# Two pairs of high and low tiles for queries and keys, and three more weight slots

## The chip, the core and the metric

The kernel runs on one core of one Trainium2 chip. The metric is the device time of one execution in microseconds (us). The engines are TensorE (PE: matmuls and transposes; PEld is its loading of weights), VectorE (DVE), ScalarE (ACT), GpSimd (POOL) and SyncE (SP), which here only issues DMAs. Each engine executes its own instructions strictly in the order in which the program lists them, so an instruction that waits holds up all that stand behind it on its engine.

## What is computed

An attention layer is followed by two feed-forward layers, all in float32. Queries, keys and values are 4 batches of 8 heads of 576 positions of 64 numbers; the attention's output is seen as 2304 tokens of 512 numbers.

```python
q_rot, k_rot = (rotate(q), rotate(k))            # cos and sin of the position
scores = scale * np.matmul(q_rot, k_rot.transpose(0, 1, 3, 2))
scores = scores - np.max(scores, axis=-1, keepdims=True)
attn = np.exp(scores)
attn = attn / (np.sum(attn, axis=-1, keepdims=True) + 1e-09)
x = np.matmul(attn, v)                           # then 2304 x 512
h = x @ w_in;  r = np.maximum(h, 0.0)            # w_in 512 x 2048
x = (s * (r * r) + b) @ w_out
g = x @ w_gate                                   # 512 x 1536
out = (g * (1.0 / (1.0 + np.exp(-g))) * (x @ w_val)) @ w_out2
```

## The kernel before

Every float32 factor is split into a high part (rounded to the format `F32R` that TensorE multiplies fast) and a low part (the rest), and a product is made of three matmuls: high by high, high by low, low by high. The high part is always made by ACT, a copy, and the low part by DVE or POOL, a subtraction.

**Attention** goes over 16 pairs of heads (`p` = 0 to 15). `prep(p)` prepares a pair: SP loads queries and keys into a tile `x` (two buffers); POOL rotates them in place (L486, L488, L491, L494); PE transposes them in three groups of three (L514) into PSUM tiles `pst`, which come from the same three PSUM buffers (`t`) as the transposes of the exponentials (L680, L683, `ps_t`); ACT writes the high parts of each group to `qkhi` (L523), and DVE the low parts to `qklo` (L525). When all three groups are done, ten DMAs on SP (L547, "the spread" below) lay `qkhi` and `qklo` out as the operands `a`, `t` and `kz` of the score matmuls. There are two sets of these operands, for even and odd pairs, so the spread of pair p can only start when the scores of pair p - 2 are done. Pairs 0 and 1 go without `qkhi` and a spread.

`pair(p)` has nine score tiles: PE multiplies (L619, `ps_s`, two PSUM buffers), DVE takes the maximum (L622, `nm`), and ACT the exponential (L626, `e`). In three thirds, the exponentials are transposed by PE, split by ACT (`ph`, L688) and DVE (`pl`, L695), and multiplied by the values (L710, L712); ACT copies the result out (L723, `xr`), and SP stores it (L731). So each pair has nine maxima on DVE and nine exponentials on ACT, by which the places in their programs are counted below.

The feed-forward weights come as 8-byte numbers. A conversion takes one ACT instruction (L304), three on DVE (L307, L310, L315), one on ACT for the high part (L342) and one for the low part (L349), on POOL for the first `WA` weights and on DVE for the others. The first `WA` weights go to slots of the pool `wa`, and they may be converted while attention still runs. When attention is done, its pools are given up, and the pool `wb` with `WB` slots takes their memory.

**The order** of the instructions comes from a planner, the class `Schedule`. Every operation has an engine, an assumed duration, a priority (a smaller number goes first) and tokens for the buffers that it takes and gives back; `sch.free` says how many buffers of each kind there are. The planner plays the program through with the assumed durations; on each engine it takes the ready operation with the best priority whose buffers are free. The chip then executes that order, with semaphores for the true dependences. The preparation of pair p has priority 100 p - 240, and unit u of pair p 100 p + 10 u. The token of `qkhi` and `qklo` is taken by the first transpose of a pair and given back when its ten spread DMAs have landed:

```python
acq = (ps_tok, hi_tok if p > 1 else tok) if g == 0 else (ps_tok,)
...
return sch.dma(
    256 * o.shape[1], lambda: nc.sync.dma_start(out=o.bitcast(F32), in_=i().bitcast(F32)), pr + 6, (*trs, *zeros[z]),
    (tok,) if first else (), (hi_tok,), pace=1.3
)
```

All DMAs of the kernel are issued on SP (`nc.sync`) and a few on ACT (`nc.scalar`), none on POOL.

Of the kernel before, what the change touches and what calls it, by code (L numbers as in the profile page):

```python
# [9 lines left out]
F32R = mybir.dt.float32r  # L10
# [154 lines left out]
def t_pool(n):  # L165
    return 2.35e-3 * n + 0.08
# [11 lines left out]
def tile_attention_moe_moe(  # L178
# [16 lines left out]
    nc = tc.nc  # L195
    B, H, S, D = q.shape
# [8 lines left out]
    NU = PC  # L205
    QA = PC // 2
    UBS = (512, 512, 512, 384, 384)
    WA = 10
    WB = 22
    NE = 7  # L210
    LATE, LAST = 1 << 20, 1 << 21
    WARM = 75
# [9 lines left out]
    sch = Schedule()  # L222
    op = sch.op
    sch.free.update({
        "raw": 3, "dec": 2, "wa": WA, "x": 2, "vr": 2, "ry": 1, "hi": 1, "vh": 3, "opb0": 1, "opb1": 1, "l": 2, "lb": 2, "cr": 1, "e": NE, "ph": 2, "pl": 2,
        "xr": 2, "rbx": 1, "s": 2, "t": 3, "v": 1, "xhb": 1, "gb": 2, "rb2": 3,
    })

# [1 line left out]
    dram = ctx.enter_context(tc.tile_pool(name="dram", bufs=1, space=DRAM))  # L230
    wa_p = ctx.enter_context(tc.tile_pool(name="wa", bufs=WA))
    raw_p = ctx.enter_context(tc.tile_pool(name="raw", bufs=3))
# [13 lines left out]
    att = ExitStack()  # L246
    at_c = att.enter_context(tc.tile_pool(name="at_c", bufs=1))
    ld_p = att.enter_context(tc.tile_pool(name="ld", bufs=2))
    vr_p = att.enter_context(tc.tile_pool(name="vr", bufs=2))
    rp_p = att.enter_context(tc.tile_pool(name="rp", bufs=1))  # L250
    v_p = att.enter_context(tc.tile_pool(name="v", bufs=3))
    ph_p = att.enter_context(tc.tile_pool(name="ph", bufs=2))
    pl_p = att.enter_context(tc.tile_pool(name="pl", bufs=2))
# [170 lines left out]
    def prep(p):  # L424
# [6 lines left out]
        st = {} if p else first_st  # L431
# [24 lines left out]
        def views2(a):  # L456
            return st["x"].rearrange("p c j (a d) -> p c j a d", a=2)[:, :, :, a], st["ry"][:, :, :, a]
# [4 lines left out]
        for g in range(G):  # L462
            cs = slice(g * PC // G, (g + 1) * PC // G)
            eng = "dve" if p == 0 else "pool"
            e = nc.vector if eng == "dve" else nc.gpsimd
            tt = t_dve if eng == "dve" else t_pool
            wide = [128, PC // G, 2, D // 2]
            def views(a, cs=cs):
                return st["x"].rearrange("p c j (a d) -> p c j a d", a=2)[:, cs, :, a], st["ry"][:, cs, :, a]
            def r0(g=g, e=e, views=views, cs=cs, wide=wide):  # L470
                if g == 0:
                    st["ry"] = rp_p.tile([128, PC, 2, 2, D // 2], F32, tag="ry", name="ry")
                e.tensor_tensor(out=views(0)[1], in0=views(1)[0], in1=rt[:, cs, 2:3].to_broadcast(wide), op=ALU.mult)
            def r1(e=e, views=views, cs=cs, wide=wide):
                e.tensor_tensor(out=views(1)[1], in0=views(0)[0], in1=rt[:, cs, 1:2].to_broadcast(wide), op=ALU.mult)
            def r2(e=e, cs=cs):
                xv = st["x"].rearrange("p c j (a d) -> p c (j a) d", a=2)[:, cs]
                e.tensor_tensor(out=xv, in0=xv, in1=rt[:, cs, 0:1].to_broadcast([128, PC // G, 4, D // 2]), op=ALU.mult)
            def r3(e=e, cs=cs):
                xv = st["x"].rearrange("p c j d -> p c (j d)")[:, cs]  # L480
                e.tensor_tensor(out=xv, in0=xv, in1=st["ry"].rearrange("p c j a d -> p c (j a d)")[:, cs], op=ALU.add)
            o = st.get("rope")
            if o is None and p:
                def y0():
                    st["ry"] = rp_p.tile([128, PC, 2, 2, D // 2], F32, tag="ry", name="ry")
                    nc.gpsimd.tensor_tensor(out=views2(0)[1], in0=views2(1)[0], in1=rt[:, :, 2:3].to_broadcast(whole), op=ALU.mult)  # L486
                def y1():
                    nc.gpsimd.tensor_tensor(out=views2(1)[1], in0=views2(0)[0], in1=rt[:, :, 1:2].to_broadcast(whole), op=ALU.mult)  # L488
                def y2():
                    xv = st["x"].rearrange("p c j (a d) -> p c (j a) d", a=2)  # L490
                    nc.gpsimd.tensor_tensor(out=xv, in0=xv, in1=rt[:, :, 0:1].to_broadcast([128, PC, 4, D // 2]), op=ALU.mult)  # L491
                def y3():
                    xv = st["x"].rearrange("p c j d -> p (c j d)")
                    nc.gpsimd.tensor_tensor(out=xv, in0=xv, in1=st["ry"].rearrange("p c j a d -> p (c j a d)"), op=ALU.add)  # L494
                n2 = PC * D
                for y, fn in enumerate((y0, y1, y2, y3)):
                    o = op("pool", t_pool(n2 if y < 2 else 2 * n2), fn, pr, (o, *lds[0], *rt_op), (ry_tok,) if y == 0 else (), (ry_tok,) if y == 3 else ())
                st["rope"] = o
            elif not p:
              o = None  # L500
              for y, fn in enumerate((r0, r1, r2, r3)):
                deps = [o, *lds[g], rt_op[g]]
                if y == 0 and g > 0:
                    deps.append(st["first"])
                o = op(eng, tt(fd if y > 1 else fd // 2), fn, pr + g, deps, (ry_tok,) if y == 0 and g == 0 else (),
                       (ry_tok,) if y == 3 else (), port=eng == "dve")
                if y == 0 and g == 0:
                    st["first"] = o
            ps_tok = Token("t")
            def tr(g=g):  # L510
                st["ps", g] = ps = ps_t.tile([128, 512], F32, tag="t", name="pst")
                rv = st["x"].rearrange("p c j d -> p c (j d)")
                for c in range(PC // G):
                    nc.tensor.transpose(taken(ps)[:, :, c * 64:(c + 1) * 64], rv[:, g * (PC // G) + c], ident.rearrange("p (h r) -> p h r", h=2))  # L514
            acq = (ps_tok, hi_tok if p > 1 else tok) if g == 0 else (ps_tok,)
            prt = pr + 3 + g
            o = st["tr"] = op("pe", 0.33, tr, prt, (o, eye_op, st.get("tr"), *(zeros[z] if p < 2 else ())), acq, (x_tok,))
            if p > 1:
                def hi(g=g):
                    if g == 0:  # L520
                        st["hi"] = rp_p.tile([128, 2 * S], F32R, tag="hi", name="qkhi")
                        st["lo"] = rp_p.tile([128, 2 * S], F32R, tag="lo", name="qklo")
                    nc.scalar.activation(out=place(st["hi"], g), in_=taken(st["ps", g]), func=AF.Copy, scale=qs_t)  # L523
                def lo(g=g):
                    nc.vector.scalar_tensor_tensor(  # L525
                        out=place(st["lo"], g), in0=taken(st["ps", g]), scalar=qs_t, in1=place(st["hi"], g).bitcast(F32), op0=ALU.mult, op1=ALU.subtract
                    )
                o = st["hi0"] = op("act", t_act(CG, True, 1), hi, prt, (o, qs_op, st.get("hi0")))
                trs.append(op("dve", t_dve(CG, 2), lo, prt, (o,), (), (ps_tok,)))
            else:  # L530
                def act(dst, rows, g=g):
                    scale = D ** -0.5 if rows is up else 1.0
                    return lambda: nc.scalar.activation(out=place(dst, g), in_=taken(st["ps", g])[rows], func=AF.Copy, scale=scale)
                def sub(dst, src, rows, g=g):
                    scale = D ** -0.5 if rows is up else 1.0
                    return lambda: nc.vector.scalar_tensor_tensor(
                        out=place(dst, g), in0=taken(st["ps", g])[rows], scalar=scale, in1=place(src, g).bitcast(F32), op0=ALU.mult, op1=ALU.subtract
                    )
                o1 = op("act", t_act(CG), act(t[dn], dn), prt, (o,))
                o2 = op("act", t_act(CG), act(a[up], up), prt, (o,))  # L540
                ops += [o1, o2, op("dve", t_dve(CG), sub(a[dn], a[up], up), prt, (o2,), (), (ps_tok,))]
                ops.append(op("act", t_act(CG), act(kz[up], dn), prt, (o,), (), (ps_tok,)))
                ops.append(op("dve", t_dve(CG), sub(t[up], t[dn], dn), prt, (o1,), (), (ps_tok,)))
# [355 lines left out]
    def switch():  # L899
        att.close()  # L900
        pool("wb", WB)

# [14 lines left out]
    n_att = len(sch.ops)  # L917
    for z in range(WA):
        weight(("out" if z % 2 else "in", z // 2), ("wa",), TP * NP, after=s_turns[WU0 + WUS * z:][:1])
    sw = op("sp", 0.0, switch, LATE - 1, [o for o in sch.ops[:n_att] if o not in ends])  # L920
    sw2 = op("sp", 0.0, switch_2, LATE - 1, [sw, *ends])
    for z in range(WA, 2 * F1):
        weight(("out" if z % 2 else "in", z // 2), ("wb", "wc"), LATE + 12 * (z - WA), sw, lo_eng="dve")

# [446 lines left out]
```

## Time and profile before

| | us |
|---|---|
| median of 3 runs | 1133.07 |
| lowest, highest | 1133.0, 1134.01 |
| span of the profiled execution | 1130.5 |
| median less that span | 2.6 |
| PE busy in the span | 1103.6 |
| DVE busy | 801.2 |
| ACT busy | 591.0 |
| POOL busy | 193.0 |

The page has no time of its own for the profiled execution but its span, from the first to the last instruction; the 2.6 us are what the median has beyond it. The scores of attention run until about 303 us of the span, and its last products with the values start at 314 us; after that only feed-forward work is left. A matmul's end is modelled in the profile, so a busy PE need not be at its peak.

### The profile page before, as it was taken

Reading aid. Unit: us, or ns where it says so; the run is one execution under the profiler, and the core shown is the slowest. Engines: PE = TensorE matmul, PEld = TensorE weight load, DVE = VectorE, ACT = ScalarE, POOL = GpSimd, SP = SyncE. Lnnn points to the kernel's source line nnn. Section 1 sums busy time; section 2 is a strip of 40 time slices with the busy share of each in tenths; the row PEclk is TensorE's granted clock in tenths of the full one; section 3 lists DMA queues with packets and bytes.
Section 4 is the critical chain, followed back from the end, with each engine's and each line's share of the span. In section 5 each row is a group of like instructions: output and inputs, shape, how many; then the busy total and the mean of one; then the engine's idle time right before and its main releaser. Section 6 shows DMA issues by size and latency. Waiting matters only on the chain. (4 is left out here: it accounts for less than half of the span.)

```text
span 1130.5 us, 17993 instructions
## 1 busy us (share of the span) xinstructions
PE 1103.6 (98%) x6314; PEld 1006.8 (89%) x6314; DVE 801.2 (71%) x1391; ACT 591.0 (52%) x1199; POOL 193.0 (17%) x156
## 2 busy tenths in 40 slices
PE   8989989999999999999999999999999999999998
PEld 7889888989988788888899999999979999899986
DVE  5879788999979867868768764555565555655560
ACT  5979888889978845544554543322242222422230
POOL 6876775752210000000000000000000000000000
PEclk9899999999999999999999999999999999999999
DMA  5587978777375477576576766766646652666501
GB/s 117 128 208 175 240 184 213 175 184 185 89 235 185 128 227 235 177 238 225 198 241 212 254 224 207 245 204 204 210 160 220 196 195 97 196 229 197 181 10 46
DMA packets 185721, 211.16 MB, mean 187 GB/s; under 512 B 71824, under 2 KB 121120, under 8 KB 185632
## 3 DMA queue, kind: packets, MB, share of 16 engines
q1 hardware_dynamic: 183792, 209.23, 61.8%
q8 instruction: 50, 0.82, 0.3%
q10 hardware_dynamic: 1840, 0.79, 0.2%
q14 instruction: 39, 0.32, 0.1%
HBM read 142.07 MB, written 47.26 MB: 167 GB/s over the span
## 5 line engine op out<-in xcount | busy, mean ns | idle before, releaser
L1241 DVE TENSOR_TENSOR tmp<-hb,tmp 128x384 f32<-128x384 f32 x252 | 140.0, 557 | 113.3 <-PE hb L811 112.4
L811 PE MATMUL hb<-xh,w 128*128 128x384 f32 (+1 forms) x560 | 199.2, 356 | 1.0 <-DVE w L349 1.0
L809 PE MATMUL hb<-xh,w 128*128 128x384 f32 (+1 forms) x560 | 199.0, 355 | 0.3 <-DVE pl L695 0.3
L810 PE MATMUL hb<-xl,w 128*128 128x384 f32 (+1 forms) x560 | 198.8, 355 | 0.0
L809 PE MATMUL acc<-gh,w 128*128 128x512 f32 (+1 forms) x320 | 117.8, 368 | 0.0
L810 PE MATMUL acc<-gl,w 128*128 128x512 f32 (+1 forms) x320 | 117.6, 368 | 0.0
L811 PE MATMUL acc<-gh,w 128*128 128x512 f32 (+1 forms) x320 | 117.6, 367 | 0.0
L622 DVE TENSOR_REDUCE nm<-ps_s 128x1 f32<-128x576 f32 x144 | 108.0, 751 | 9.8 <-PE ps_s L619 8.6
L809 PEld LDWEIGHTS hb<-xh,w 128*128 128x128 f32 x560 | 105.1, 188 | 10.9 <-PE ps_t L683 0.5
L810 PEld LDWEIGHTS hb<-xl,w 128*128 128x128 f32 x560 | 105.1, 188 | 10.3
L811 PEld LDWEIGHTS hb<-xh,w 128*128 128x128 f32 x560 | 105.1, 188 | 9.8 <-DVE w L349 1.8
L626 ACT ACTIVATE e<-ps_s,nm 128x576 f32<-128x576 f32 x144 | 107.3, 746 | 8.4 <-DVE nm L622 7.8
L688 ACT ACTIVATE ph<-ps_t 128x512 fp32r<-128x512 f32 x192 | 106.2, 574 | 10.1 <-PE ps_t L680 7.8
L619 PE MATMUL ps_s<-t,a 128*128 128x288 f32 x320 | 101.2, 332 | 7.2 <-ACT e L626 7.0
L710 PE MATMUL ps_av<-ph,vh 128*128 128x384 f32 (+1 forms) x320 | 97.9, 327 | 0.7 <-ACT xr L723 0.6
L695 DVE TENSOR_TENSOR pl<-ps_t,ph 128x512 fp32r<-128x512 f32 x144 | 95.9, 683 | 2.5 <-ACT ph L688 1.4
L1256 ACT ACTIVATE tmp<-tmp 128x384 f32<-128x384 f32 x72 | 37.8, 525 | 111.1 <-DVE tmp L1241 108.9
L680 PE MATMUL ps_t<-ident,e 128*128 128x128 f32 x576 | 87.7, 279 | 5.6 <-DVE qklo L525 4.0
L619 PE MATMUL ps_s<-kz,a 128*128 128x288 f32 x320 | 90.8, 299 | 0.0
L810 PE MATMUL hb<-w 128*128 128x384 f32 x264 | 88.9, 337 | 0.0
L811 PE MATMUL hb<-w 128*128 128x384 f32 x264 | 88.8, 337 | 0.0
L809 PE MATMUL hb<-w 128*128 128x384 f32 x264 | 88.5, 335 | 0.0
(117 smaller groups left out, 2304.2 us busy)
## 6 DMA issues: line engine op xcount, KB each, us to landing
w<-wd SPq DMA_DIRECT2D x120, 512.0 KB, 4.3
wd<-w SPq DMA_DIRECT2D x48, 512.0 KB, 3.6
raw<-in_moe_w_out_dram SPq DMA_DIRECT2D x28, 512.0 KB, 4.1
x_d<-xr SPq DMA_DIRECT2D x64, 144.0 KB, 2.7
w<-wd SPq DMA_DIRECT2D x36, 256.0 KB, 3.6
raw<-in_moe_w_in_dram SPq DMA_DIRECT2D x16, 512.0 KB, 4.4
raw<-in_moe_w_gate_dram SPq DMA_DIRECT2D x12, 512.0 KB, 5.5
raw<-in_moe_w_val_dram SPq DMA_DIRECT2D x12, 512.0 KB, 6.6
```

Of the source, the lines that this page charges most:

```text
L619: nc.tensor.matmul(ps[:, hf * 512:hf * 512 + HS], a[:, q0:q0 + 128], m[:, k0:k0 + HS], start=y == 0, stop=y == len(todo) - 1)
L622: nc.vector.tensor_reduce(out=st["nm"][:, u:u + 1], in_=st["s", u], axis=AX.XY, op=ALU.max, negate=True)
L626: nc.scalar.activation(out=st["e", u].rearrange("p (f n) -> p f n", f=2), in_=st["s", u], func=AF.Exp, bias=st["nm"][:, u:u + 1], accum_ou ...
L680: nc.tensor.transpose(ps[:, z * 128:z * 128 + 128], st["e", u][:, kc * 128:kc * 128 + 128], ident)
L688: nc.scalar.activation(out=st["ph", y][0:rows, 512 * i:512 * i + n], in_=st["pt", y, i][0:rows, 0:n], func=AF.Copy)
L695: nc.vector.tensor_tensor(out=dst, in0=st["pt", y, i][0:rows, 0:n], in1=st["ph", y][0:rows, c].bitcast(F32), op=ALU.subtract)
L710: nc.tensor.matmul(ps, vv, st["ph", y][:, c], start=kc == 0, stop=kc == 4)
L809: nc.tensor.matmul(o, lh, rh, start=first, stop=False)
L810: nc.tensor.matmul(o, lh, rl, start=False, stop=False)
L811: nc.tensor.matmul(o, ll, rh, start=False, stop=last)
L1241: nc.vector.tensor_tensor(out=st[dst, f], in0=ps[z], in1=st[a, f], op=ALU.add)
L1256: nc.scalar.activation(out=st[key, f], in_=st[key, f], func=AF.Silu)
```

## The change

The tiles `qkhi` and `qklo` move from the pool `rp` (one buffer) to a pool `hi` of their own with two buffers each, and the planner's count of them goes from 1 to 2. The pool `wa` gets 11 slots in place of 10, and `wb` 24 in place of 22. The memory comes from `dynamic_dma_scratch_size`, by which the program keeps 1 KB of each partition for DMA descriptors in place of 16. A pair of `qkhi` and `qklo` has 9 KB of a partition, a weight slot 4 KB. From line 251 on, lines of the changed kernel have a number that is higher by one.

```diff
-    WA = 10
-    WB = 22
+    WA = 11
+    WB = 24
...
-        "raw": 3, "dec": 2, "wa": WA, "x": 2, "vr": 2, "ry": 1, "hi": 1, "vh": 3, "opb0": 1, "opb1": 1, "l": 2, "lb": 2, "cr": 1, "e": NE, "ph": 2, "pl": 2,
+        "raw": 3, "dec": 2, "wa": WA, "x": 2, "vr": 2, "ry": 1, "hi": 2, "vh": 3, "opb0": 1, "opb1": 1, "l": 2, "lb": 2, "cr": 1, "e": NE, "ph": 2, "pl": 2,
...
     rp_p = att.enter_context(tc.tile_pool(name="rp", bufs=1))
+    hi_p = att.enter_context(tc.tile_pool(name="hi", bufs=2))
...
-                        st["hi"] = rp_p.tile([128, 2 * S], F32R, tag="hi", name="qkhi")
-                        st["lo"] = rp_p.tile([128, 2 * S], F32R, tag="lo", name="qklo")
+                        st["hi"] = hi_p.tile([128, 2 * S], F32R, tag="hi", name="qkhi")
+                        st["lo"] = hi_p.tile([128, 2 * S], F32R, tag="lo", name="qklo")
...
-    nc = _bacc.Bacc("TRN2", target_bir_lowering=False, num_devices=1)
+    nc = _bacc.Bacc("TRN2", target_bir_lowering=False, num_devices=1, dynamic_dma_scratch_size=1024)
```

Since the planner has other counts, it gives out another order in all of attention. On ACT, before, the three parts of `qkhi` of pair 8 (`qkhi_2047`) stand around the fifth exponential of pair 6 (the exponentials with `nm_1908`):

```order
L626 ACTIVATE e_1966,l_1371<-ps_s_1930,nm_1908 128x576
L688 ACTIVATE ph_1960<-ps_t_1968 128x512
L688 ACTIVATE ph_1960<-ps_t_1978 128x512
L626 ACTIVATE e_1998,l_1371<-ps_s_1955,nm_1908 128x576
L626 ACTIVATE e_2015,l_1371<-ps_s_1989,nm_1908 128x576
L723 ACTIVATE xr_1928<-ps_av_1941 128x384
L688 ACTIVATE ph_1960<-ps_t_2017 64x384
L523 ACTIVATE qkhi_2047<-pst_2037,qs_203 128x2x192
L523 ACTIVATE qkhi_2047<-pst_2043,qs_203 128x2x192
L626 ACTIVATE e_2066,l_1371<-ps_s_2021,nm_1908 128x576
L523 ACTIVATE qkhi_2047<-pst_2050,qs_203 128x2x192
L688 ACTIVATE ph_2088<-ps_t_2073 128x512
```

On ACT of the changed kernel, `qkhi` of pair 8 (`qkhi_1845`) stands around the seventh exponential of pair 5 (`nm_1642`):

```order
L627 ACTIVATE e_1764,l_1393<-ps_s_1736,nm_1642 128x576
L724 ACTIVATE xr_1697<-ps_av_1709 128x384
L689 ACTIVATE ph_1707<-ps_t_1767 64x384
L689 ACTIVATE ph_1803<-ps_t_1791 128x512
L627 ACTIVATE e_1811,l_1393<-ps_s_1775,nm_1642 128x576
L689 ACTIVATE ph_1803<-ps_t_1815 128x512
L627 ACTIVATE e_1832,l_1393<-ps_s_1798,nm_1642 128x576
L524 ACTIVATE qkhi_1845<-pst_1835,qs_206 128x2x192
L524 ACTIVATE qkhi_1845<-pst_1841,qs_206 128x2x192
L627 ACTIVATE e_1866,l_1393<-ps_s_1826,nm_1642 128x576
L524 ACTIVATE qkhi_1845<-pst_1854,qs_206 128x2x192
L724 ACTIVATE xr_1697<-ps_av_1787 128x384
```

So it moved ahead by seven of the nine exponentials of a pair. From pair 7 to 15 it is seven for every pair, within one, and the nine transposes on PE and the three `qklo` on DVE move with it.

On DVE, before, the end of the last pair's maxima (`nm_4327`) has two instructions of weight conversions among twelve:

```order
L622 TENSOR_REDUCE nm_4327<-ps_s_4456 128x1
L695 TENSOR_TENSOR pl_4476<-ps_t_4450,ph_4461 128x512
L310 SCALAR_TENSOR_TENSOR dec_4316<-raw_4046,dec_4316 128x512
L695 TENSOR_TENSOR pl_4476<-ps_t_4468,ph_4461 128x512
L622 TENSOR_REDUCE nm_4327<-ps_s_4479 128x1
L695 TENSOR_TENSOR pl_4476<-ps_t_4487,ph_4461 128x512
L622 TENSOR_REDUCE nm_4327<-ps_s_4496 128x1
L307 TENSOR_SCALAR dec_4448<-dec_4448 128x512
L695 TENSOR_TENSOR ph_4461<-ps_t_4503,ph_4461 64x384
L695 TENSOR_TENSOR pl_4541<-ps_t_4508,ph_4531 128x512
L622 TENSOR_REDUCE nm_4327<-ps_s_4534 128x1
L695 TENSOR_TENSOR pl_4541<-ps_t_4525,ph_4531 128x512
```

In the changed kernel the same place on DVE (`nm_4351`) has three:

```order
L316 SCALAR_TENSOR_TENSOR dec_4390<-raw_4067,dec_4390 128x512
L696 TENSOR_TENSOR pl_4500<-ps_t_4474,ph_4482 128x512
L623 TENSOR_REDUCE nm_4351<-ps_s_4484 128x1
L696 TENSOR_TENSOR pl_4500<-ps_t_4493,ph_4482 128x512
L623 TENSOR_REDUCE nm_4351<-ps_s_4503 128x1
L696 TENSOR_TENSOR pl_4500<-ps_t_4511,ph_4482 128x512
L308 TENSOR_SCALAR dec_4452<-dec_4452 128x512
L311 SCALAR_TENSOR_TENSOR dec_4452<-raw_4324,dec_4452 128x512
L623 TENSOR_REDUCE nm_4351<-ps_s_4531 128x1
L696 TENSOR_TENSOR ph_4482<-ps_t_4522,ph_4482 64x384
L623 TENSOR_REDUCE nm_4351<-ps_s_4554 128x1
L696 TENSOR_TENSOR pl_4580<-ps_t_4544,ph_4559 128x512
```

Counted over the whole of attention, 8, 7 and 6 instructions of L307, L310 and L315 stand ahead of the last maximum before, and 10, 10 and 9 now; ahead of the last `pl` or `ph` of attention (L695) they are 10, 9 and 9 before, and 11, 11 and 11 now.

## Rows read from the trace of the kernel before

**Rows 1.** Page, span and section 1: busy us, share of span, instructions.

```profile
span 1130.5 us, 17993 instructions
PE 1103.6 (98%) x6314; PEld 1006.8 (89%) x6314; DVE 801.2 (71%) x1391; ACT 591.0 (52%) x1199; POOL 193.0 (17%) x156
```

**Rows 2.** Stretches: length, then PE, PEld, DVE, ACT, POOL busy us.

```profile
51.00:200.00 149.00, 137.78 (x1052) 128.86 (x1051) 127.84 (x205) 125.47 (x299) 102.37 (x79) 1.00 0.83 201
200.00:303.00 103.00, 101.36 (x765) 94.46 (x765) 100.53 (x161) 93.93 (x222) 48.88 (x41) 1.00 0.69 164
400.00:450.00 50.00, 50.00 (x217) 40.31 (x216) 37.43 (x68) 24.66 (x42) 0.00 (x0) 1.00 0.68 218
1000.00:1131.00 131.00, 124.81 (x644) 114.82 (x643) 63.69 (x120) 28.86 (x58) 0.00 (x0) 0.99 0.38 121
```

**Rows 3.** PE's waits in 51 to 200 us: total, times, longest.

```profile
PE ps_t L680 <- DVE qklo L525: 4.0, 2, 2.6
PE ps_s L619 <- ACT e L626: 3.4, 4, 2.0
PE pst L514 <- DVE qklo L525: 1.9, 1, 1.9
PE psr L646 <- DVE qklo L525: 0.9, 1, 0.9
```

**Rows 4.** Groups by line, 51 to 200 us: busy, mean ns, idle before.

```profile
L523 ACT ACTIVATE qkhi<-pst,qs 128x384 fp32r<-128x384 f32 x27 | 15.1, 582 | 14.7 <-DMA x_d<-xr 4.6 <-DMA kz<-qkhi 4.0 <-PE pst L514 2.3
L525 DVE SCALAR_TENSOR_TENSOR qklo<-pst,qs,qkhi 128x384 fp32r<-128x384 f32 x27 | 16.0, 613 | 12.8 <-ACT qkhi L523 10.1 <-DMA x_d<-xr 1.8 <-DMA rbx<-r_d 0.9
```

**Rows 5.** The same view, 200 to 303 us.

```profile
L525 DVE SCALAR_TENSOR_TENSOR qklo<-pst,qs,qkhi 128x384 fp32r<-128x384 f32 x12 | 7.2, 612 | 0.5 <-ACT qkhi L523 0.3
```

**Rows 6.** Timeline, 131 to 150 us: start, duration, engine, line.

```profile
132.37 0.60 SPq L547 DMA_DIRECT2D kz<-qkhi  x1
...
134.70 2.63 POOL L494 TENSOR_TENSOR x<-x,ry 128x1152 f32<-128x1152 f32 x1
...
135.20 1.05 ACT L523 ACTIVATE qkhi<-pst,qs 128x384 fp32r<-128x384 f32 x2 [4.01 <-DMA kz<-qkhi]
135.82 1.15 DVE L525 SCALAR_TENSOR_TENSOR qklo<-pst,qs,qkhi 128x384 fp32r<-128x384 f32 x2 [3.25 <-ACT qkhi L523]
...
136.49 1.18 PE L680 MATMUL ps_t<-ident,e 128*128 128x128 f32 x8 [2.63 <-DVE qklo L525]
...
143.01 0.38 PE L619 MATMUL ps_s<-t,a 128*128 128x288 f32 x1
...
149.81 0.38 PE L514 MATMUL pst<-ident,x 128*128 128x128 f32 x2
```

**Rows 7.** Stretches, maxima (L622) alone: length, DVE busy, count.

```profile
51.00:200.00 149.00, 53.71 (x72) 1.00 0.83 201
200.00:303.00 103.00, 40.06 (x54) 1.00 0.69 164
```

**Rows 8.** Groups by line, DVE and ACT, 51 to 303 us.

```profile
L310 DVE SCALAR_TENSOR_TENSOR dec<-raw,dec 128x512 uint32<-128x512 uint32 x7 | 5.1, 728 | 0.0
L315 DVE SCALAR_TENSOR_TENSOR dec<-raw,dec 128x512 uint32<-128x512 uint32 x6 | 4.8, 817 | 0.0
L307 DVE TENSOR_SCALAR dec<-dec 128x512 uint32<-128x512 uint32 x8 | 3.5, 442 | 0.3 <-ACT dec L304 0.3
...
L304 ACT ACTIVATE dec<-raw 128x512 f32<-128x512 f32 x8 | 5.5, 692 | 1.1 <-DMA raw<-in_moe_w_out_dram 1.1
L342 ACT ACTIVATE w<-dec 128x512 fp32r<-128x512 f32 x6 | 3.8, 639 | 0.5 <-DVE dec L315 0.5
```

**Rows 9.** L798, 51 to 303 and 303 to 420 us: ns min/median/max.

```profile
L798 DVE TENSOR_TENSOR xl<-xs,xh x4: 618/978/1656, 150.2 to 207.8; 128x512 fp32r<-128x512 f32 x4
L798 DVE TENSOR_TENSOR xl<-xs,xh x5: 682/683/685, 344.1 to 416.3; 128x512 fp32r<-128x512 f32 x5
```

**Rows 10.** PE's waits in 303 to 1131 us.

```profile
PE hb L811 <- DVE w L349: 1.0, 2, 0.5
```

## Prediction

> **What bounds the kernel now.** I read the page's busy times first, then the same by stretches, then PE's waits, and then the rows around the tiles that the change doubles. The span is 1130.5 us, in which PE is busy 98% [rows 1]. The stretches tell two kernels apart. From 400 us on PE is busy all the time (50.00 of 50.00), and DVE and ACT have room; only the last stretch loses some (124.81 of 131) [rows 2]. There, nothing but fewer matmuls would help, and the change has as many as before. In attention, PE has gaps, and DVE and ACT are nearly as busy as PE. From 200 to 303 us DVE is busy 100.53 of 103 us (97.6%): it is the bound. From 51 to 200 us it is busy only 127.84 of 149 (86%), ACT 125.47 (84%), PE 137.78 (92%) [rows 2]: none is full, so something makes them wait for one another. The pace says the same: 72 maxima in 149 us are 8 pairs at 18.6 us, 54 in 103 us are 6 pairs at 17.2 us [rows 7], and PE starts 1052 matmuls in the one and 765 in the other [rows 2], 7.06 and 7.43 per us.
>
> What they wait for is in the rows of the changed tiles. In 51 to 200 us ACT sits idle 14.7 us ahead of `qkhi`, 4.6 and 4.0 of them until a DMA landed, and DVE 12.8 us ahead of `qklo`, 10.1 of them for ACT [rows 4]; 12.8 are 60% of DVE's 21.2 us of idle time. The timeline shows one case word for word. The last spread DMA of pair 7 is issued at 132.37 us; ACT, ready 4.01 us earlier, starts `qkhi` of pair 8 at 135.20, DVE starts `qklo` at 135.82 after 3.25 us, and PE, whose next transposes need the PSUM buffer that `qklo` reads, at 136.49 after 2.63 us [rows 6]. So one pair of `qkhi` and `qklo` is still being read by the DMAs of pair 7 when pair 8 wants to write it, and the wait goes through all three engines. PE's own rows give 4.0 + 1.9 + 0.9 = 6.8 us that `qklo` ended, and 3.4 us that exponentials ended, part of them held up behind `qkhi` on ACT [rows 3].
>
> **The second pair of tiles.** It removes that wait: `qkhi` of pair p then waits for the spread of pair p - 2. The order on ACT moves `qkhi` ahead by seven exponentials, 7/9 of a pair, or 14.5 us at 18.6 us a pair, while the DMAs that it needs are a whole pair older. So it has 18.6 - 14.5 = 4.1 us more than before, and the longest wait of ACT was 4.0 us [rows 4, 6]: nearly all of these waits should go. The spread itself is not sped up: it still waits for the scores of pair p - 2. Nor does it have to be: pair 7's last spread DMA is issued at 132.37 us and its scores start at 143.01 [rows 6]. What the waits are worth is bounded from both sides. Below: PE's 6.8 us, if nothing else gets better. Above: DVE's 12.8 us, and 0.5 in the second stretch [rows 4, 5], 13.3 in all, if DVE works through all of it. Between lie the pace of PE (1052 matmuls at 7.43 per us are 141.6 us, 7.4 less) and that of the pairs (8 times 1.4 us, 11.5 less, with the two stretches' other work not quite alike). I take 10: three quarters of 13.3, since in a chain of three engines a removed wait partly comes back as a shorter one, and DVE would then be busy 127.84 of 139, 92%, still less than the 97.6% that it reaches where these waits are few (0.5 us [rows 5]). **Term: -10.**
>
> **The third thing that the planner did: more conversions inside attention.** With another weight slot and freer engines it puts weight conversions earlier. Until the last maximum there are 2 more of L307 and 3 more of L310 and L315: 2 x 0.44 + 3 x 0.73 + 3 x 0.82 = 5.5 us of DVE; until the end of attention's last subtraction, 1, 2 and 2 more: 3.5 us [rows 8]. ACT gets 3 x (0.69 + 0.64) = 4.0 us [rows 8]. In 200 to 303 us DVE has only 2.5 us to spare [rows 2], so this is paid there. It is hardly given back: after attention PE waits for weights 1.0 us in all [rows 10]. Bounds are 0, if the conversions fall into idle time, and 5.5; I take 3.5, what is left when the last conversions only change places at the end. **Term: +3.5.**
>
> Here the trace shows something that speaks against the change. The subtraction L798, with two inputs in SBUF, takes 618 to 1656 ns, median 978, while POOL is busy in attention, and 682 to 685 after it [rows 9]. The Trainium skill has the rule (SBUF — State Buffer, section Who interferes with whom): VectorE with two SBUF inputs and GpSimd share a pair of ports under an exclusive lock, and the one that comes second waits for the other's whole instruction. The trace agrees, with 1656 against 683 ns. L310 and L315 have two such inputs too; their means in attention, 728 and 817 ns, hold what this cost them so far [rows 8], so the term above has it. By the longest case each of the six would take 1656 - 683 = 973 ns more, 5.8 us.
>
> **The slots and the scratch.** Two more slots after attention let loads start earlier; the only wait that they could shorten is that 1.0 us [rows 10]. Term: 0, at best -1. One low part moves from DVE to POOL, which is idle after attention. The scratch could matter only if DMA issues got longer by it. No DMA is issued on POOL, and an issue on SP takes 0.60 us; ten issues 50% longer would be 3 us, and a spread has 10.6 us between its last issue and its use [rows 6]. Term: 0. The Trainium skill (DMA: Bandwidth & Descriptors, section SWDGE vs HWDGE vs iDMA) says that only DMAs issued from GpSimd keep their descriptors in a ring in SBUF; no run shows it yet, and it gives the same 0.
>
> **Sum.** 1130.5 + 2.6 = 1133.1 us, less 10, plus 3.5: **1126.6 us**.
>
> **Rivals.**
>
> *The wait passes on to the rotation.* Pair 9's rotation ends at 134.70 + 2.63 = 137.33 us and its first transpose starts at 149.81: 12.5 us of room [rows 6], less than the 14.5 by which transposes move. If the loads of `x` and POOL stay where they are, each of 8 pairs starts 2 us late, and PE waits for POOL: 8 x 2.0 = 16 would eat everything. But a load waits only for the transposes two pairs before, which move too, so the lag is paid at the start, one or two pairs, 3 to 4 us: 1126.6 + 3.5 = 1130.1.
>
> *DVE is the bound anyway.* If the waits only come back as others, PE gets its lower bound of 6.8, and conversions cost 5.5: 1131.8, or with some more lost 1133.5. For it speaks DVE's 97.6% in the second stretch, against it that the first has 21.2 us of idle time.
>
> *Slower.* Nothing is won in 51 to 200 us, since the order is planned with durations that the chip does not keep, and the conversions stand in front of attention's work on DVE in 200 to 303 us: 5.5 us, and up to 5.8 more if each meets a POOL instruction as the longest L798 did: 1138.6 to 1144.4. It decides from the point where less than 5.5 us of waits are won.
>
> *The change doesn't do what it says.* 2.3 of ACT's 14.7 us ended with transposes, not a DMA [rows 4]; if the transposes were what comes late, 1133 would stay. The case at 135.20, with transposes long done, is against it.
>
> **How the numbers follow.** A difference of 0.2% is 2.3 us, about what a measurement of this kernel can tell from no change. Chances: the forecast 0.70, with its own range from 1119 (13.3 and the saved 1.0 won, no conversion felt) to 1131.8 (6.8 won, 5.5 paid); rotation 0.08, half of it over the bound; DVE 0.10, no change; slower 0.08; no effect 0.04. Faster: 0.70 + 0.04 and 0.01 of DVE's case, 0.75. Same: 0.04 + 0.09 + 0.03, 0.16. Slower: 0.09. The range leaves out the slower case and the far end: 1118.5 to 1133.
>
> **What would show it.** Right: ACT's idle time ahead of `qkhi` and DVE's ahead of `qklo` fall below 3 us each over attention; PE has no wait on `qklo` over 1 us; DVE's busy share in the first 150 us after 51 rises over 90%; the scores end at about 297 us in place of 303, and all after it shifts by the same. Wrong: idle time ahead of L514 that a POOL instruction ends (rotation); DVE at 97% from early on with an unchanged pace (DVE the bound); L310 and L315 over 1 us on average (the ports); or loads that are issued late on SP, which would show as POOL's waits for `x`.

## The result, and the profile after

The changed kernel takes 1141.18 us (median of 6 runs, 1137.55 to 1146.94), the kernel before 1133.33 beside it: 1.0072 times as long, interval 1.0051 to 1.0092. It is slower, where the prediction had 1126.6 us and gave "slower" 0.09. The scores of attention end at 308.6 us of the profiled execution, before at 303.1, where the prediction had about 297.

First the page of the changed kernel, as [rows 1]: span, then busy us, share and count of each engine.

```profile
span 1140.0 us, 17979 instructions
PE 1104.6 (97%) x6314; PEld 1009.2 (89%) x6314; DVE 800.5 (70%) x1390; ACT 593.8 (52%) x1199; POOL 192.3 (17%) x157
```

The engines do the same work in the same busy time; the span is 9.5 us longer. Next the stretches of [rows 2], with one more from 303 to 320 us (after the count of each engine stands the granted clock as a share of full speed, the DMA share and GB/s):

```profile
51.00:200.00 149.00, 134.88 (x1029) 127.21 (x1028) 128.23 (x202) 123.67 (x292) 100.40 (x76) 0.98 0.81 197
200.00:303.00 103.00, 97.64 (x740) 91.26 (x739) 98.55 (x159) 94.06 (x221) 52.03 (x45) 1.00 0.69 174
303.00:320.00 17.00, 13.66 (x90) 12.25 (x89) 14.59 (x25) 12.50 (x29) 3.82 (x3) 0.87 0.13 29
400.00:450.00 50.00, 50.00 (x219) 40.65 (x218) 31.50 (x58) 25.78 (x42) 0.00 (x0) 1.00 0.60 191
```

From 400 us on PE is busy all the time, as before. Over both stretches of attention together, 51 to 303 us, PE, DVE and ACT are all busy less than before (232.5, 226.8 and 217.7 us, before 239.1, 228.4 and 219.4), and from 200 to 303 us DVE too has more idle time (98.55 of 103, before 100.53). So the loss is in attention, and it is waiting, not work. When it arises is read from the matmuls that PE has started by three times. Of the kernel before:

```profile
0.00:125.00 125.00, 115.82 (x913) 109.22 (x913) 100.89 (x166) 98.58 (x229) 85.38 (x70) 0.96 0.71 170
0.00:200.00 200.00, 183.08 (x1417) 171.03 (x1418) 163.77 (x265) 160.21 (x375) 138.10 (x112) 0.97 0.75 180
0.00:320.00 320.00, 301.14 (x2275) 279.73 (x2276) 277.48 (x446) 268.94 (x626) 193.03 (x156) 0.98 0.72 174
```

Of the changed kernel:

```profile
0.00:125.00 125.00, 118.36 (x950) 111.79 (x951) 105.65 (x174) 103.52 (x240) 87.81 (x69) 0.97 0.70 167
0.00:200.00 200.00, 179.64 (x1401) 168.60 (x1402) 165.40 (x265) 159.20 (x370) 136.41 (x110) 0.97 0.74 178
0.00:320.00 320.00, 290.94 (x2226) 272.11 (x2227) 278.53 (x446) 265.76 (x617) 192.25 (x157) 0.97 0.69 169
```

By 125 us the changed kernel is 37 matmuls ahead (950 against 913; 8 of them were ahead at 51 us already). By 200 it is 16 behind, by 320 it is 49 behind. So 53 are lost from 125 to 200 us, and 33 more from 200 to 320. What 49 are worth goes by the pace of the kernel before from 450 to 1000 us, 5.16 per us:

```profile
450.00:1000.00 550.00, 548.60 (x2837) 507.20 (x2836) 355.64 (x640) 206.45 (x371) 0.00 (x0) 1.00 0.63 207
```

They are 9.5 us, the whole difference of the spans. So the second pair of tiles did at first what it was to do, and all of it and more was lost after 125 us.

Where, the waits tell. PE in 51 to 200 us, as [rows 3]:

```profile
PE ps_t L681 <- DVE qklo L526: 8.8, 2, 8.6
PE ps_t L681 <- DVE ph L696: 2.4, 1, 2.4
PE ps_s L620 <- ACT e L627: 1.9, 1, 1.9
```

And the tiles' groups in that stretch, as [rows 4]:

```profile
L524 ACT ACTIVATE qkhi<-pst,qs 128x384 fp32r<-128x384 f32 x26 | 14.5, 584 | 9.9 <-DMA x_d<-xr 9.0 <-DMA kz<-qkhi 0.5 <-PE pst L515 0.2
L526 DVE SCALAR_TENSOR_TENSOR qklo<-pst,qs,qkhi 128x384 fp32r<-128x384 f32 x26 | 15.3, 610 | 10.1 <-DMA x_d<-xr 8.9 <-ACT qkhi L524 1.1
```

Ahead of `qkhi` ACT is idle 9.9 us, before 14.7. But before, the idle time was spread over many waits, the longest 4.0 us; now it is one wait of 9 us, and nearly all the rest is gone. The profile names a store, `x_d`, as what ended the wait; it infers that, and the store is only a DMA issued around that time. What `qkhi` of pair 9 needs by the program is that the spread of pair 7 has landed, since it takes that pair's tiles. The timeline of SP shows that this spread was late (first the end of pair 5's scores on PE, after which it may start; then SP's issues):

```profile
117.27 0.29 PE L620 MATMUL ps_s<-kz,a 128*128 128x288 f32 x1
...
117.31 0.44 SPq L762 DMA_DIRECT2D xh<-x_d  x1
117.84 1.61 SPq L732 DMA_DIRECT2D x_d<-xr  x2
119.50 0.69 SPq L447 DMA_DIRECT2D vr<-in_v_dram  x1
...
127.17 1.11 SPq L778 DMA_DIRECT2D rbx<-r_d  x2
128.39 0.59 SPq L393 DMA_DIRECT2D x<-in_q_dram  x1
129.02 0.73 SPq L393 DMA_DIRECT2D x<-in_k_dram  x1
129.80 1.31 SPq L548 DMA_DIRECT2D a<-qkhi  x1
...
136.28 0.60 SPq L548 DMA_DIRECT2D kz<-qkhi  x1
```

The operands are free from 117.56 us on, and the spread starts at 129.80, 12.2 us later, behind the stores, five loads of values, the loads of the first feed-forward tokens (L762, L778) and those of pair 10. In the kernel before, the same two events were 4.5 us apart:

```profile
121.42 0.29 PE L619 MATMUL ps_s<-kz,a 128*128 128x288 f32 x1
126.17 0.59 SPq L547 DMA_DIRECT2D a<-qkhi  x1
```

For L778 SP itself stood still 3.5 us, until the token load issued at 117.31 had landed:

```profile
SPq L778 <- DMA xh<-x_d: 3.5, 1, 3.5
```

L778 reads nothing that the token load brings. In the trace SP's DMAs use eight semaphores in turn, and the issue at 127.17 waits for the semaphore of the DMA eight issues before it, which is that load. So SP is held up not only by issuing, but also when the eighth DMA before is slow to land.

The last spread DMA goes out at 136.28, and then the stall ends, on ACT, DVE and PE in turn:

```profile
140.44 1.05 ACT L524 ACTIVATE qkhi<-pst,qs 128x384 fp32r<-128x384 f32 x2 [8.99 <-DMA x_d<-xr]
141.05 1.14 DVE L526 SCALAR_TENSOR_TENSOR qklo<-pst,qs,qkhi 128x384 fp32r<-128x384 f32 x2 [8.94 <-DMA x_d<-xr]
141.72 0.69 PE L681 MATMUL ps_t<-ident,e 128*128 128x128 f32 x2 [8.64 <-DVE qklo L526]
```

The clock adds to it. The stretches around the stall, all columns as above:

```profile
125.00:132.70 7.70, 7.70 (x63) 7.46 (x62) 5.92 (x10) 5.12 (x13) 6.59 (x6) 1.00 0.74 166
132.70:141.40 8.70, 0.38 (x3) 0.10 (x1) 0.35 (x1) 0.96 (x3) 7.25 (x7) 0.81 0.95 234
141.40:145.00 3.60, 3.28 (x14) 3.14 (x15) 3.14 (x6) 3.10 (x9) 3.60 (x3) 0.51 0.41 94
145.00:152.00 7.00, 7.00 (x59) 6.85 (x58) 5.96 (x10) 5.91 (x15) 4.24 (x5) 1.00 1.02 236
```

During the stall the granted clock falls, and in the first 3.6 us of work after it is 0.51 (the level of 1.2 GHz): 14 matmuls, where 59 in 7 us (30 in 3.6) are usual. A second place of the kind is at the end of attention, where [rows 2] have no stretch: DVE's L311, a weight conversion with two inputs in SBUF, meets a POOL instruction (1.75 us, on average 0.73), L316 follows (0.62), DVE is late with `ph`, and PE waits.

```profile
312.74 1.27 POOL L350 TENSOR_TENSOR w<-dec,w 128x512 fp32r<-128x512 f32 x1 [6.52 <-ACT w L343]
312.81 1.75 DVE L311 SCALAR_TENSOR_TENSOR dec<-raw,dec 128x512 uint32<-128x512 uint32 x1
...
316.03 0.53 PE L711 MATMUL ps_av<-ph,vh 128*128 128x192 f32 x1 [2.64 <-DVE ph L696]
```

Behind that gap the clock is 0.50 again from 315.6 to 322.4 us, with 25 matmuls in 6.8 us, and 36 in the 7.6 that follow:

```profile
315.60:322.40 6.80, 6.37 (x25) 6.01 (x26) 2.90 (x5) 2.29 (x5) 1.27 (x1) 0.50 0.20 45
322.40:330.00 7.60, 7.60 (x36) 6.42 (x36) 1.16 (x3) 4.78 (x8) 0.00 (x0) 1.00 0.86 255
```

These two places are not all of it. From 200 to 303 us, between them, 25 of the 33 matmuls are lost (740 against 765). From 200 to 320 us PE waits 4.2 us in all for exponentials, before 0.7, in waits of at most 1.7 us; what makes these late was not taken apart.

### The profile page after: what moved, and what is told of

It reads as the page before. It is cut to its first block, busy times and chain, and to the rows that moved or that the text cites. A ratio compares the mean times of both kernels' runs of the same rounds, so it can differ in the third digit from the quotient of the medians.

```text
span 1140.0 us, 17979 instructions
## 1 busy us (share of the span) xinstructions
PE 1104.6 (97%) x6314; PEld 1009.2 (89%) x6314; DVE 800.5 (70%) x1390; ACT 593.8 (52%) x1199; POOL 192.3 (17%) x157
## 4 chain that ended last, share of the span: by engine, by line
PE 85%; DVE 7%; ACT 3%; SPq 2%; DMA 1%; issue 1%; POOL 0%; ACTq 0%; POOLq 0%; DVEq 0%
PE hb L812 14%; PE hb L811 14%; PE hb L810 14%; PE acc L811 6%; PE acc L810 6%; PE acc L812 6%; PE acc L1174 4%; PE acc L1175 4%; PE ps_s L620 4%; PE acc L1176 4%; PE ps_t L681 3%; PE ps_av L711 2%; DVE pl L696 2%; DVE nm L623 2%; PE ps_av L713 2%
## 5 line engine op out<-in xcount | busy, mean ns | idle before, releaser
L627 ACT ACTIVATE e<-ps_s,nm 128x576 f32<-128x576 f32 x144 | 106.7, 742 | 11.5 <-DVE nm L623 10.0
L711 PE MATMUL ps_av<-ph,vh 128*128 128x384 f32 (+1 forms) x320 | 101.9, 339 | 3.7 <-DVE ph L696 2.6
```

Of the source, the lines that this page charges most:

```text
L627: nc.scalar.activation(out=st["e", u].rearrange("p (f n) -> p f n", f=2), in_=st["s", u], func=AF.Exp, bias=st["nm"][:, u:u + 1], accum_ou ...
L711: nc.tensor.matmul(ps, vv, st["ph", y][:, c], start=kc == 0, stop=kc == 4)
```

## The experiments

The theory: the tiles are good, the slots and the scratch do nothing, and what costs is the new order that the planner gave out with two tiles, because SP, which issues DMAs for 127.0 of the 149 us from 51 to 200 in the kernel before (199 DMAs of 638 ns; summed from the timeline), cannot serve that order in time. The rivals: the tiles are worth nothing; the slots or the smaller scratch do harm; or two pairs of tiles are too few. Ratios are to the kernel before on the same chip, with a 95% interval. The times are medians, but each trace is of one execution, and some of these lie far from their medians: those of e1 (1144.18 us), e7 (1137.69) and e10 (1136.35) are the longest of their kernels, 4.6 to 7.0 us over the median, that of e9 (1137.71) is the second longest, 3.1 over it, and those of e3 (1126.61) and e11 (1123.61) are the shortest, 2.8 and 1.2 under it.

**Tiles without slots, slots without tiles.** `e1_tiles_only`, the change with the old slots:

```diff
-    WA = 11
-    WB = 24
+    WA = 10
+    WB = 22
```

> The second pair of tiles and the smaller scratch, with 10 and 22 weight slots as before; the order of attention is the changed kernel's up to its last pair. Theory 'late spread' (the changed kernel loses its time where ACT waits 9.0 us for the spread of pair 7, which SP issues 12 us after pair 5's scores have ended): the same stall of 8 to 10 us ahead of qkhi of pair 9, and 1138 to 1143 us. Rival 'slots' (conversions and slots cost it): no such loss, at most 1134.

1137.18 us, 1.0047 (1.0023 to 1.0072): slower, by the tiles and the order alone. The stall stands at the same place, 6.8 us ahead of `qkhi` of pair 9; time and stall are both a little under what was expected (1138, and 8 us). In the profiled execution there is another stall, on DVE:

```profile
212.05 7.25 DVE L799 TENSOR_TENSOR xl<-xs,xh 128x512 fp32r<-128x512 f32 x1
...
216.13 2.63 POOL L495 TENSOR_TENSOR x<-x,ry 128x1152 f32<-128x1152 f32 x1
...
221.50 0.61 PE L620 MATMUL ps_s<-t,a 128*128 128x288 f32 x1 [5.93 <-ACT e L627]
```

`e2_slots_only` is the kernel before with 11 and 24 slots and the 1 KB of scratch, one pair of tiles:

```diff
-    WA = 10
-    WB = 22
+    WA = 11
+    WB = 24
...
-    nc = _bacc.Bacc("TRN2", target_bir_lowering=False, num_devices=1)
+    nc = _bacc.Bacc("TRN2", target_bir_lowering=False, num_devices=1, dynamic_dma_scratch_size=1024)
```

> 11 and 24 weight slots and the smaller scratch, with one pair of tiles as before. Theory 'late spread': about as before, 1131 to 1136 us, waits ahead of qkhi as before (12 to 18 us on ACT). Rival 'slots': 1138 us or more. Rival 'scratch' (DMA issues get longer with 1 KB): mean issue time on SP over 0.7 us in 51 to 200 us, and slower than 1136.

1131.2 us, 0.9988 (0.9974 to 1.0002): no difference that can be measured. SP's issues take 647 ns on average, 638 before. Under the old order, slots and scratch are out. Under the new one, what they are worth is the difference of the changed kernel and e1 (1.0072 and 1.0047), and these intervals overlap.

**Tiles without the new order.** `e3_two_tiles_old_order` has both pairs in memory (and the old slots), but the planner counts one, so every engine gets the order of the kernel before; in the two traces it is the same on all engines, instruction by instruction. It differs from `e1_tiles_only` in this one number:

```diff
-        ... "ry": 1, "hi": 2, "vh": 3, ...
+        ... "ry": 1, "hi": 1, "vh": 3, ...
```

> Two pairs of tiles in memory, but the planner still counts one: every engine has the order of the kernel before, instruction by instruction, and only the wait for the tiles is gone; 10 and 22 slots, the smaller scratch. If the waits are worth what the prediction says: idle time ahead of qkhi under 3 us, 10 us won, 1123 us. Theory 'late spread': SP issues for 127 of 149 us in 51 to 200 us, so spreads soon come late and half or less of it is won, 1126 to 1130. Rival 'scratch': slower than 1133.

1129.36 us, 0.997 (0.9955 to 0.9986): faster, with the same tiles. No wait of `qkhi` on a DMA is left, and scores end at 297.6 us in the profiled execution, the shortest of ten, where the prediction had about 297. But the median is only 3.4 us less, not 10: another late thing now stands out.

```profile
ACT xh L797 <- POOL xs L793: 7.9, 2, 6.6
ACT qkhi L524 <- PE pst L515: 5.2, 6, 2.1
```

ACT waits up to 6.6 us for the first tokens' sums (POOL, with rows that SP loads late, L778), and PE behind it 4.2 us at 152.73. In the kernel before this wait is 1.4 us in all; with the waits ahead of `qkhi` gone, ACT comes to the tokens earlier, and their sums don't.

**Three pairs.** `e4_three_tiles`, the change with three buffers (and 9 and 22 slots, for room); the planner still counts two:

```diff
-    hi_p = att.enter_context(tc.tile_pool(name="hi", bufs=2))
+    hi_p = att.enter_context(tc.tile_pool(name="hi", bufs=3))
```

> Three pairs of tiles in memory where the planner counts two (one weight slot less, 9, to make room; order of attention as in the changed kernel up to the last pair). Theory 'late spread': the 9 us ahead of qkhi of pair 9 are gone, but the spread of pair 7 is still late, so now the scores of pair 7 wait for it, some 4 to 5 us; 1132 to 1137. Rival 'order' (the moved conversions and preparations cost it everywhere): 1139 or more.

1136.11 us, 1.0041 (1.0024 to 1.0059). The 9 us wait is gone, as a third pair must do, and more than half of the loss is not: the spread of pair 7 still starts 11.7 us after pair 5's scores. The scores of pair 7 wait for it 1.6 us, not 4 to 5 as expected; the longest wait is now that of ACT for the tokens (5.5 us, PE 4.2 behind it). Every engine has the order of the changed kernel until about 291 us. So a late spread without the stall on the tiles still goes with a loss.

**Less work for SP.** In the kernels of this part the second halves of `t` and `kz` are spread together with the first, 7 DMAs in place of 10:

```diff
...
+                w = slice(0, 2 * S)
-                ops.append(sp(t[64:128, c], lambda c=c: st["hi"][64:128, c]))
+                ops.append(sp(t[64:128, c], lambda: st["hi"][64:128, w], put=None if s0 else t[64:128, w]))
...
```

(and so for `t[0:64]` and `kz`; with `put=None` the operation stays in the plan and issues nothing). `e5_fewer_spreads` is the changed kernel with this, `e6_old_order_fewer` is e3 with it, `e8_before_fewer` the kernel before with it.

> The changed kernel with every engine's order kept, but the spread is 7 DMAs in place of 10 (the two halves of t and kz go in one DMA each; same bytes): 42 issues fewer on SP. Theory 'late spread' (SP cannot issue the spread of pair 7 when pair 5's scores are done, since it is late with what stands ahead): the spread starts some 2 us earlier and is 2 us shorter, so ACT's wait ahead of qkhi of pair 9 falls from 9 to 4 to 6 us; 1134 to 1138 us against 1141. Rival 'order' (SP has nothing to do with it): no change from the changed kernel, 1139 or more.

> Two pairs of tiles in memory with the planner's count of one (the order of before on every engine, 10 and 22 slots), and the spread in 7 DMAs. With ten DMAs this order ran 3.5 us faster than before, with a wait of 6.6 us of ACT for the tokens of the first feed-forward block, whose loads stand on SP. Theory 'SP late': that wait gets shorter too, 1 to 3 us more, 1126 to 1129. Rival (POOL's own work is what comes late there): no change, 1129 to 1131.

> The kernel before, its own order and one pair of tiles, with the spread of a pair issued as 7 DMAs and not as 10 (SP issues 42 fewer, at a mean of 638 ns 27 us less of issuing over the whole attention). If the gain of e6 (0.9938) came from SP's load alone, this run gives it too: about 1125 to 1127 us. If it takes both (the second pair of tiles takes the wait for the landing away, and SP has room for what then comes earlier), this run stays within 0.3% of before, 1129 to 1134, since the conversions still wait for the spread one pair before; a spread that lands 1.3 to 2 us earlier shortens those waits by no more than a third (3 us of 10).

e5: 1139.31 us, 1.0066 (1.0045 to 1.0087). The wait ahead of `qkhi` of pair 9 falls as the theory said, from 9.0 to 5.2 us:

```profile
ACT qkhi L524 <- DMA kz<-qkhi: 5.2, 1, 5.2
```

The time does not follow: 1134 to 1138 was expected, and 1139.31 is in the range of the rival, "1139 or more", with a ratio that can't be told from the changed kernel's 1.0072. So SP's load sets the length of the stall, and this run does not show that the stall is what the time is lost by. e6: 1126.3 us, 0.9938 (0.9917 to 0.9960), as expected; but ACT's wait for the tokens, which was to get shorter, is still 6.3 us. e8: 1131.3 us, 0.9989 (0.998 to 0.9999): almost nothing, as expected if it takes both. So the tiles are worth 0.5% between e8 and e6, and 0.3% with SP as loaded as before (e3).

**The tokens later, and a planner that knows the issues.** In `e7_tokens_later` the changed kernel's first token loads depend on the start of pair 8's scores too; in `e9_issue_time` the planner takes 0.65 us for a DMA issue in place of 0.55 (and as much more in two other lines that set it):

```diff
+        if i == 0:
+            deps.append(s_turns[9 * 8])
```

```diff
-        o = self.op(eng, 0.55, fn, prio, deps, acq, rel)
+        o = self.op(eng, 0.65, fn, prio, deps, acq, rel)
```

> The changed kernel, where the loads of the first feed-forward block's tokens (two of 1 MB and sixteen of sums) may only start once the scores of pair 8 have begun; the planner makes a new order for what follows. Theory 'late spread': nothing big stands ahead of the spread of pair 7, it starts within 4 us of the end of pair 5's scores, and ACT's wait of 9 us is gone; 1129 to 1135, unless the burst does the same to a later pair. Rival 'order' (the preparations are placed too early for POOL and the loads of x): the wait stays at pair 9 or turns into PE's wait for transposes; 1139 or more.

> The changed kernel, where the planner takes 0.65 us for a DMA's issue on SP in place of 0.55 (the runs show 0.62 to 0.65 on average): it then sees SP fall behind and makes another order (the tokens' loads come after the spread of pair 7). Theory 'SP late': no wait over 4 us ahead of qkhi; 1127 to 1134. Rival 'order': 1138 or more.

e7: 1132.79 us, 0.9999 (0.9983 to 1.0014). e9: 1134.61, 1.0024 (1.0005 to 1.0042). e7 is in its range, e9 0.6 us over its own. Both take away the 9 us stall (3.4 us in two waits, and 2.9 in one, ahead of `qkhi`) and most of the loss; neither wins anything over the kernel before. In e7, up to 151 us of the changed kernel's time, PE, DVE and ACT keep its order; until the stall only SP's differs, from the token loads at 116.24 on, and POOL's, from the tokens' sums at 129.06. e9 has another order from the start. In the profiled execution of e7 the next late thing is a weight that SP loads, in front of ACT's own work:

```profile
ACT dec L305 <- DMA raw<-in_moe_w_in_dram: 6.7, 1, 6.7
```

In that of e9 it is DVE against POOL, as in e1 but longer:

```profile
203.45 1.46 POOL L487 TENSOR_TENSOR ry<-x,rt 128x576 f32<-128x576 f32 x1
...
204.75 9.19 DVE L799 TENSOR_TENSOR xl<-xs,xh 128x512 fp32r<-128x512 f32 x1
...
207.47 2.67 POOL L492 TENSOR_TENSOR x<-x,rt 128x1152 f32<-128x1152 f32 x1
...
210.73 2.66 POOL L495 TENSOR_TENSOR x<-x,ry 128x1152 f32<-128x1152 f32 x1
...
215.53 0.61 PE L620 MATMUL ps_s<-t,a 128*128 128x288 f32 x1 [7.17 <-ACT e L627]
```

`e10_fewer_and_later` has the 7 DMAs of e5 and the later tokens of e7.

> The changed kernel with both reliefs of SP: 7 spread DMAs (e5) and the first token loads only after the start of pair 8's scores (e7). If the loss comes from SP being late for the spread of pair 7 and the half clock behind that stall, this run has no wait over 3 us ahead of qkhi between 100 and 200 us, scores end by 302, and the time is 1127 to 1132. If the order that the planner chose is worse by itself (its conversions and weights put between the scores), it stays at 1132 to 1139, with waits of several us at other places.

1131.71 us, 0.9997 (0.9986 to 1.0007). The time is in the first range, and no wait over 0.6 us ahead of `qkhi` is left. In the profiled execution, the longest of twelve and 4.6 us over the median, scores end at 306.4 us, not by 302, with a 4.3 us wait of ACT for a weight's load (PE waits 4.2 behind it) and DVE's L311 and L316 held up to 3.2 and 3.1 us. So both halves of that expectation are partly right: with SP relieved, and the order that the planner gives out then, the loss is gone, and nothing is won over the kernel before.

**The best of it.** `e11_old_order_all` has the whole change (two pairs, 11 and 24 slots, 1 KB) and the 7 DMAs, and the planner counts one pair. It differs from e5 in that one number alone.

> e6 with the 11 and 24 weight slots of the change: all of the change except the order of the attention's work, and 7 DMAs per spread. The attention's order stands as in e6, the order behind it differs. As e2 showed the slots to be worth nothing (0.9988), 1124 to 1128 us, as e6. If more slots let weights come early enough to matter behind the attention, up to 2 us less.

1124.82 us (1123.61 to 1126.5), 0.9937 (0.9925 to 0.9948), faster than both kernels. Against e5 (1.0066 on its chip) one number in the planner makes 14.5 us. Its first stretch:

```profile
51.00:200.00 149.00, 142.12 (x1094) 135.80 (x1092) 132.27 (x212) 130.22 (x311) 107.67 (x82) 0.99 0.87 207
```

and the tiles in it:

```profile
L526 DVE SCALAR_TENSOR_TENSOR qklo<-pst,qs,qkhi 128x384 fp32r<-128x384 f32 x27 | 15.9, 608 | 5.7 <-ACT qkhi L524 5.6
L524 ACT ACTIVATE qkhi<-pst,qs 128x384 fp32r<-128x384 f32 x27 | 15.0, 581 | 4.8 <-PE pst L515 4.7
```

PE starts 1094 matmuls from 51 to 200 us, before 1052, 7.34 per us: nearly the 7.43 of the second stretch, which the prediction took as what could be reached. One stall is left, ACT with the tokens:

```profile
ACT xh L798 <- POOL xs L794: 5.1, 1, 5.1
```

`e12_old_order_later` tries to take that away, with the later tokens of e7.

> The version of e11 with the first block's tokens loaded only after the start of pair 8's scores, as in e7. In e11 the only stall over 3 us left between 51 and 310 us is one of 4.3 us, where ACT waits 5.1 us with a token copy for sums that POOL makes from rows that SP loads late, with a half clock behind it. If that wait costs what it shows and nothing takes its place, 3 to 5 us less than e11, 1120 to 1122 us. If another late thing takes its place, as in e7 and e10 (a weight's load), 1123 to 1127, as e11. The planner's order of the attention changes with it in part, so more than that is not told apart.

1128.57 us, 0.9953 (0.9938 to 0.9967): a miss on both ranges. The wait splits in three (6.2 us in sum, the longest 3.1), and in 51 to 200 us PE starts 1076 matmuls, 18 fewer than in e11. As the plan changes with this edit, what it costs by itself stays open.

## Why the prediction was wrong

*The waits that were to go.* "Nearly all of these waits should go" held but for one place, after 125 us. The step that failed is the margin: "it has 18.6 - 14.5 = 4.1 us more than before", with "nor does it have to be" on the speed of the spread. That took the spread's own lateness as fixed. In the kernel before, the spread whose last DMA is in [rows 6] begins at 126.17 us, 4.5 us after pair 5's scores. SP's queue stood in the same new order as the others, and in it the spread came 12.2 us after those scores: 7.7 us later than before, more than the margin. Its last DMA also took longer from its issue to the start of `qkhi`, 4.16 us in place of 2.83 [rows 6]. Worked out from these, 4.0 - 4.1 + 7.7 + 1.3 is an estimate of 8.9 us for the wait; ACT shows 9.0. The ten DMAs were weighed against 10.6 us up to the scores, the wrong user: their first user, with two pairs of tiles, is `qkhi` of pair 9. The prediction had read the busy share of PE, DVE, ACT and POOL, and not SP, which issues 127.0 of 149 us and is the fullest but PE and DVE. It did name the sign, POOL's waits for `x` behind late loads on SP, but gave it no price.

*The size.* -10 us was mis-sized by itself, too. With the order held, the tiles give 3.4 us (e3), and in its trace ACT's wait for the tokens takes the place of the wait for the tiles; with SP relieved, 5.8 us more than the relief alone (0.9938 against 0.9989 of 1131 us), and scores that end at 296.0 (e6). The prediction's upper and lower bounds (6.8 and 13.3) both lay above that. (The pace of the pairs, 8 times 1.4, is 11.2 there and not 11.5; the term does not hang on it.)

*The conversions.* +3.5 us has no measurement of its own. There are more of them in the changed order, about as forecast (from 51 to 303 us 9, 9 and 8 of L308, L311 and L316, in [rows 8] 8, 7 and 6), 17.9 us of DVE in place of 13.4. But DVE is less busy from 200 to 303 us, not fuller, so they did not fill it up there as the prediction said; whether one of them in front of a maximum holds PE up there is not shown. Nor did the sign for the ports come, a mean over 1 us: L311 and L316 take 0.73 us each. The one case in which such conversions are seen to cost is at 312.81, L311 with 1.75 us against POOL and L316 behind it, with a PE wait of 2.6 and the half clock behind that.

*The slots and the scratch.* 0 was right (e2, 0.9988; e11 against e6, 0.9937 against 0.9938). The Trainium skill (DMA: Bandwidth & Descriptors, section SWDGE vs HWDGE vs iDMA) has the descriptor rings in SBUF only on the path of DMAs issued from GpSimd. e2 agrees: with a sixteenth of the scratch an issue on SP takes 647 ns, 638 before.

*The rivals.* "Slower" named 1138.6 to 1144.4 us, and the time fell there, but by another way: its ground was DVE filled up with conversions from 200 to 303 us, and DVE is 95.7% busy there, before 97.6%. "The order is planned with durations that the chip does not keep" was its other half, and e9 agrees with it: with 0.65 in place of 0.55 us for an issue the planner's order is 0.5% faster. The rotation was late as well in the changed kernel (POOL waits 12.2 us for `x` from 100 to 141 us), and no experiment takes it apart from the spread, since both stand in SP's queue. But it did not end the 9 us stall: POOL is done with pair 9 at 128.27, and PE starts its transposes at 130.88, before ACT stops.

*What is shown and what is not.* That the order costs, and not the tiles, is shown twice by one number (e1 against e3, e5 against e11). That SP's lateness makes the 9 us stall is shown by e7, which takes the token loads out of SP's way and loses the stall with the order of PE, DVE and ACT unchanged until then, and by e5, which only issues fewer DMAs and shortens it to 5.2. One rival stays: the token loads are 2 MB, and e7 and e10 take these bytes off the DMA engines as well as the issues off SP; e5, with the same bytes, is only part of an answer. What the stall is worth in time is not shown: e5 and e4, which keep the order of attention (e4 until 291 us), win back 0.1 and 0.3% of the 0.7, and e7 and e10, which win back all of it, have another order behind it. What makes the order no better than before even then is only read from single profiled executions, and those of e1, e7, e9 and e10 are of the long ones: a late weight load in front of ACT's work, DVE held up by POOL, and a half clock behind each. They change places from kernel to kernel, and no run takes one away alone.

## What to carry to other kernels

A second buffer is two changes where a planner counts buffers: the memory that takes a wait away, and a new order on all engines. Try the first alone, under the old order; here it was worth 0.3 to 0.5%, and the new order cost 0.8 to 1.3%. And before a margin is taken as given, count the busy time of the queue that issues the DMAs, and look for each DMA's first user: here an in-order queue that issued for 85% of the time came 7.7 us later than before to work that was asked for earlier.

## What the hardware showed that was not expected

A DVE instruction with two SBUF inputs can be held up through a whole row of POOL instructions. L799 took 9.19 us in e9 while POOL ran from L487 at 203.45 to the end of L495 at 213.39, and 7.25 us in e1; alone it takes 0.68 [rows 9]. The Trainium skill (SBUF — State Buffer, section Who interferes with whom) has an exclusive lock that is held for a whole instruction; here the wait lasted until POOL paused, longer than any one of its instructions (2.67 us), so the prediction's worst case of 0.97 us for each conversion was no bound.

A gap on PE cost more than its length, twice in the changed kernel. After the gap of 8.6 us the clock stood at half for the next 3.6 us of work, and after one of 2.6 us for 6.8, with 3.7 matmuls started per us there against 4.7 in the 7.6 us behind it.
